# Two transformer layers on one core: the exchange of routed rows in two stages, the first during the output projection

## The chip, the core and the metric

The kernel runs on one NeuronCore of a Trainium2 chip. The core has five engines, each with its own in-order queue of instructions: PE (TensorE, matrix products; PEld is its weight load), DVE (VectorE), ACT (ScalarE), POOL (GpSimd) and SP (SyncE, which here only starts transfers). They wait for one another by semaphores, and 16 DMA engines move data between DRAM and on-chip memory. The metric is the device time of one execution in microseconds (us). Over three runs the kernel before took 4654.71 us in the median, from 4647.03 to 4658.94.

## The reference

Two equal layers over `x` of 2048 tokens by 1024 features, all in float32. A layer is attention and then a feed-forward network on eight routed tokens:

```python
def _A_ref(x, wqkv, wo):                     # attention, 32 heads of 32
    q, k, v = (x @ wqkv) split into heads
    p = softmax(einsum("bhqd,bhkd->bhqk", q, k) * 32 ** -0.5)
    return einsum("bhqk,bhkd->bhqd", p, v) merged @ wo

def _B_ref(x, w_r, w_gate, w_up, w_down):    # routed feed-forward
    r = x @ w_r                              # one score per token
    idx = argsort(-r)[:8]                    # the eight tokens with the highest score
    x_sel = x[idx]
    y = (silu(x_sel @ w_gate) * (x_sel @ w_up)) @ w_down * sigmoid(r[idx])
    return x with y added at the rows idx

x = x + _A_ref(_layernorm(x), ...);  x = x + _B_ref(_layernorm(x), ...)   # layer 1
x = x + _A_ref(_layernorm(x), ...);  x = x + _B_ref(_layernorm(x), ...)   # layer 2, same weights
```

So layer 2 needs all rows of layer 1, and eight of them only after layer 1's feed-forward network, which in turn can only begin when all 2048 scores are known.

## The kernel before, in words

**Products in halves.** TensorE works in a reduced type (fp32r) here. To keep accuracy each operand of the projections is split into a high half, a rounded copy made by ACT, and a low half, the operand minus its high half, made by POOL or DVE. Each product is three passes: high by high, low by high, high by low.

**One layer.** `layer(n, src, dst, prev)` is called with n = 0 and n = 1 (below: layer 1 and layer 2).

1. *Projection.* The tokens go in 4 chunks `c` of 512, the weight `wqkv` in 12 blocks `wb` of 256 columns (0 to 3 queries, 4 to 7 keys; 8 to 11 values, where a pair of blocks halves the sum). That gives 48 blocks and 96 half-block steps `k`; the first chunk takes the value blocks first, the others last. `load_w` fetches a raw block into `wraw`, `split_w` makes `wh` on ACT (line 584) and `wl` on POOL (line 585), two buffers of each. The loop emits the split of block j+1, and the load of block j+2, at the first step of block j (lines 741 to 745). A token tile of 128 rows is loaded by SP (`xt`), measured (`ln_stats`, lines 133 to 138) and normalised (`ln_norm`, line 599) on DVE and POOL, transposed by PE (line 612), and copied to `xh` by ACT (line 613) and `xl` by DVE (line 617). The products are line 634. ACT copies a query or key step's result out at line 648, a value block's at line 675, and DVE makes the low half after it.
2. *Attention.* 32 units (8 groups of 4 heads by 4 query chunks) of 16 key tiles each. The keys of the first group are fetched by `load_k`, at the steps that `KEYS_AT` names.
3. *Output projection.* 16 token tiles. `ord` (attention output and reciprocal sums), its halves `ohl`, and the split weights `woh` and `wol` feed 48 products per tile (line 991). Then DVE adds the residual, normalises, and reduces with `w_r` to the tile's column of scores (line 1019); POOL adds (line 1020), and SP stores the tile to `dst`.
4. *Routing.* During tile 15, `candidates` finds the best eight of the first 15 tiles; `route` adds the last tile's and settles the eight.
5. *Feed-forward.* Weight pieces of 1 MB (`fw`) are fetched by `load`, and `FeedForward.steps` holds 49 steps: gate (`g`) and up (`u`) products, 8 pieces each for two halves of the columns, transposes, 14 down products, and the sum `y`.

**Between the layers.** `dst` of layer 1 is a DRAM buffer, `x3`. Layer 2 must not wait for the feed-forward network. So `exchange` moves the routed rows out of the way: it works out which of the last eight rows are not routed themselves, gathers them and scatters them to the places of the routed rows further ahead (lines 240 and 241, through `gather`, line 199, and `scatter`, line 203). From then on the last eight rows of `x3` belong to the routed tokens, and only layer 2's last token tile waits for the network. Attention over all tokens does not depend on their order; at the end `back` moves rows to their own places, and `token` translates row numbers.

Layer 2's start is written out by hand: load two blocks of weights and the first three tiles, split block 0, five feed-forward steps with the gate's products held back (`hold`), statistics and norms, four more feed-forward steps, then transposes of tiles 0 and 1. In the loop, `k % 4 == 2` brings three more feed-forward steps (`tick`, which also sends off the loads that the steps before it have made room for), line 731. At k=60 the network is done and layer 2's last tile is loaded.

The order on each engine is the order in which the program emits, engine by engine; buffers of one name in a pool are reused in turn, and an instruction that needs a buffer waits until its earlier users are done.

Of the kernel before, what the change touches and what calls it, by code (L numbers as in the profile page):

```python
# [27 lines left out]


# [13 lines left out]
KEYS_AT = {(2, 23): slice(0, 3 * 512), (3, 3): slice(3 * 512, S)}  # L43
# [14 lines left out]
def tile_kernel(ctx, tc, x, wqkv, wo, w_r, w_gate, w_up, w_down, out):  # L58
# [49 lines left out]
    tail = cons.tile([128, 8], F32, name="tail")  # L108
    pool.iota(pos, pattern=[[128, NT]], base=0, channel_multiplier=1, allow_small_or_imprecise_dtypes=True)
    pool.iota(tail, pattern=[[1, 8]], base=S - 8, channel_multiplier=0, allow_small_or_imprecise_dtypes=True)  # L110
# [9 lines left out]
    pool.iota(last_c, pattern=[[0, 9]], base=S - 128, channel_multiplier=1, allow_small_or_imprecise_dtypes=True)  # L120
    ones16 = cons.tile([NT, 128], F32, name="ones16")
    pool.memset(ones16, 1.0)
    ones_c = ones16[0:8]
    PERM = {}
# [16 lines left out]
    class FeedForward:  # L141
# [5 lines left out]

        def __init__(self, n, dst, mrd):
            self.n, self.dst, self.mrd = n, dst, mrd
            self.stacks, self.pools, self.W, self.HT, self.t = [], [], {}, {}, {}  # L150
            self.todo, self.steps, self.free = [], [], []
            for h in range(2):
                for k in "gu":
                    self.steps += [(k, h, a) for a in range(KD)]
                self.steps.append(("t", h, 0))
            self.steps += [("d", 0, c) for c in range(14)] + [("y", 0, 0)]
            self.todo = [u for u in self.steps if u[0] in "gud"]
            self.lag, self.hold, self.late = 0, False, None
# [9 lines left out]
        def open(self):  # L168
# [4 lines left out]
            else:  # L173
                self.fx = self.push("fwa", 5, "right")
                self.pools = [(self.push("fwb", 4, "right"), "fw", 4)] * 4 + [(self.fx, "fw", 5)] * len(self.todo)
# [26 lines left out]
        def scatter(self, idx, in_):  # L202
            pool.indirect_dma_start(out=self.dst, out_offset=bass.IndirectOffsetOnAxis(ap=idx[:, :1], axis=0),
                                    in_=in_, in_offset=None)
# [4 lines left out]
        def exchange(self, sb, idx):  # L209


            tiny = self.tiny
            s, tcol = sb[:, 0:1], self.tcol
            lt, ne, ni, nit = tiny([8, 1], "lt"), tiny([8, 8], "ne"), tiny([8, 1], "ni"), tiny([8, 1], "nit")
            dve.tensor_scalar(lt, s, float(S - 8), None, op0=OP.is_lt)
# [4 lines left out]
            dve.tensor_tensor(nit, ni, tcol, op=OP.mult)  # L220
            p = ps_st()
# [4 lines left out]
            dve.tensor_scalar(eq, p[0:8, 8:16], d, None, op0=OP.is_equal)  # L226
            p = ps_st()
            pe.matmul(p[0:8, 0:1], eq, nit, start=True, stop=True)
            v = tiny([8, 4], "v")
# [7 lines left out]
            abi = PERM["ab"] = cons.tile([8, 2], I32, name="abi")  # L237
            dve.tensor_copy(abi, ab)
            tg = self.tmp.tile([128, D], F32, name="x", bufs=3)[0:8]
            self.gather(tg, abi[:, 0:1], self.dst)  # L240
            self.scatter(abi[:, 1:2], tg)
            dve.tensor_copy(v[:, 0:1], s)
            self.v = v

        def permutation(self):

            p = ps_st()
            for i in range(3):
                vb = small.tile([8, 128], F32, name="vb")
                pool.tensor_scalar(vb, ones_c, self.v[:, i:i + 1], None, op0=OP.mult)  # L250
                pe.matmul(p[:, 8 * i:8 * i + 8], vb, ident[0:8, 0:8], start=True, stop=True)
            bc = PERM["bc"] = cons.tile([128, 24], F32, name="bc")
            dve.tensor_copy(bc, p[:, 0:24])

        def back(self):

            rows, last = (self.tmp.tile([128, D], F32, name=i, bufs=k)[0:8] for i, k in (("x", 3), ("wrb", 1)))
            self.gather(rows, PERM["ab"][:, 1:2], self.dst)
            act.dma_start(last, self.dst[S - 8:S, :])
            self.scatter(PERM["ab"][:, 0:1], rows)  # L260
            self.scatter(PERM["routed"], last)

        def token(self, idx, s):

            a, b, bc = self.tiny([8, 1], "ta"), self.tiny([8, 1], "tb"), PERM["bc"]
            j = small.tile([8, 8], F32, name="tj")
            dve.scalar_tensor_tensor(j, bc[0:8, 0:8], s, bc[0:8, 8:16], op0=OP.is_equal, op1=OP.mult, accum_out=a)
            dve.scalar_tensor_tensor(j, tail[0:8], s, bc[0:8, 16:24], op0=OP.is_equal, op1=OP.mult, accum_out=b)
            dve.tensor_tensor(a, a, b, op=OP.add)
            dve.tensor_tensor(a, a, s, op=OP.add)  # L270
            dve.tensor_copy(idx, a)
# [46 lines left out]
        def route(self, rcols, xn, wp):  # L318


            n, tiny = self.n, self.tiny
            self.tmp = wp
            self.bg = bg = wp.tile([128, D], F32, name="x", bufs=3)[0:8] if n else self.fx.tile([8, D], F32, name="bg", bufs=1)
            xs = self.xs = (self.fs if n else self.fx).tile([128, KD, 32], F32, name="xs", bufs=1)
            pool.memset(xs, 0.0)
            if not n:
                self.tcol = tiny([8, 1], "tcol")
                pool.tensor_scalar(self.tcol, pos[0:8, 0:1], float(S - 8), None, op0=OP.add)
# [5 lines left out]
            mx, mi, mif = tiny([1, 8], "mx"), tiny([1, 8], "mi", U32), tiny([1, 8], "mif")  # L334
# [5 lines left out]
            pick = tiny([128, 2, 8], "pick2")  # L340
# [3 lines left out]

            def tokens():
                p = ps_st()
                pe.matmul(p[0:8, 0:9], pl, last_c, start=True, stop=False)
                pe.matmul(p[0:8, 0:9], pc, self.ca, start=False, stop=True)
                if not n:
                    pe.matmul(p[0:8, 16:24], last_c[:, 0:8], pl, start=True, stop=False)  # L350
                    pe.matmul(p[0:8, 16:24], self.ca[:, 0:8], pc, start=False, stop=True)
                sb = tiny([8, 24], "sb")
                for sl in (slice(0, 9), slice(16, 24))[:2 - n]:
                    dve.tensor_copy(sb[:, sl], p[0:8, sl])
                idx = tiny([8, 1], "idx", I32) if n else cons.tile([8, 1], I32, name="routed")
                dve.tensor_copy(idx, sb[:, 0:1])
                self.gather(bg, idx, self.dst)
                return sb, idx

            if not n:  # L360
                sb, PERM["routed"] = tokens()
                self.exchange(sb, idx=PERM["routed"])
# [7 lines left out]
            if n:  # L370
                sb, idx = tokens()
                self.back()
                self.tok = tiny([8, 1], "tok", I32)
                self.token(self.tok, sb[:, 0:1])
# [3 lines left out]
            dve.reciprocal(sg, sg)  # L378

        def row_tile(self):  # L380
            return self.tmp.tile([128, D], F32, name="xn", bufs=1) if self.n else self.fx.tile([128, D], F32, name="fy", bufs=1)

        def gate(self):
            if self.late:
                e, g = self.late
                self.late = None
                dve.tensor_scalar(e, e, 1.0, None, op0=OP.add)
                dve.reciprocal(e, e)  # L388
                pool.tensor_tensor(e, g, e, op=OP.mult)

        def step(self):
# [6 lines left out]
            if k in "gu":  # L398
# [6 lines left out]
                if a == KD - 1:  # L405
                    acc = self.acc
                    if k == "g":
# [4 lines left out]
                        self.late = (e[:m], g[:m])  # L412
                        if not self.hold:
                            self.gate()
# [23 lines left out]
            else:  # L438
# [5 lines left out]
                if self.n:  # L444
                    self.scatter(self.tok, self.bg)
                else:
                    dma(self.dst[S - 8:S, :], self.bg)
# [4 lines left out]
        def tick(self):  # L452
            for _ in range(self.lag):
                self.load()
            self.lag = self.step()

        def finish(self):
            while self.steps:
                if self.step():
                    self.load()  # L460
            self.close()

        def close(self):
# [3 lines left out]
            if self.n:  # L467
                self.end.close()

    def layer(n, src, dst, prev=None):  # L470
# [6 lines left out]
        mrd = dram.tile([S, 2], F32, name=f"mrd{n}")  # L477
# [83 lines left out]
        with ExitStack() as pst:  # L561
# [16 lines left out]
            def split_w(parts=1):  # L578
                wb, raw = RAW.pop(0)
                wh, wl = (pr_.tile([128, 2048], F32R, name=i) for i in ("wh", "wl"))  # L580
                W[wb] = [w.rearrange("p (a c) -> p a c", a=KD if wb < 8 else 4) for w in (wh, wl)]
                for i in range(parts):
                    sl = slice(2048 // parts * i, 2048 // parts * (i + 1))
                    act.copy(wh[:, sl], raw[:, sl])  # L584
                    pool.tensor_tensor(wl[:, sl], raw[:, sl], wh[:, sl].bitcast(F32), op=OP.subtract)  # L585
                    yield

            def ln_load(t):
                XT[t] = pr_.tile([128, D], F32, name="xt", bufs=3)
                dma(XT[t], src[t * 128:(t + 1) * 128, :])  # L590
# [10 lines left out]
            def ln_tr(t, wide=True):  # L601
                c, i = divmod(t, 4)
                if i == 0:
                    XC[c] = (pw.tile([128, KD, 512], F32R, name="xh"), pw.tile([128, KD, 512], F32R, name="xl"))
                xh, xl = XC[c]
                sl = slice(i * 128, (i + 1) * 128)
                ps = [(slice(0, KD), ps_pre())] if wide else [(slice(4 * j, 4 * j + 4), ps_st()) for j in range(2)]
                ps = [(asl, p.rearrange("p (a c) -> p a c", c=128)) for asl, p in ps]
                for asl, p in ps:
                    for j in range(asl.stop - asl.start):  # L610
                        a = asl.start + j
                        pe.transpose(p[:, j, :], XT[t][:, a * 128:(a + 1) * 128], ident)
                    act.copy(xh[:, asl, sl], p)

                def low():
                    for asl, p in ps:
# [445 lines left out]
```

## Time and profile before

One profiled execution took 4656.52 us, and its span from the first to the last instruction was 4654.5 us. All durations below are of this execution.

| what | value |
| --- | --- |
| median of three runs | 4654.71 us (4647.03 to 4658.94) |
| profiled execution / its span | 4656.52 / 4654.5 us |
| busy share PE, PEld | 98%, 58% |
| busy share DVE, POOL, ACT | 68%, 69%, 52% |
| mean granted TensorE clock | 0.987 |
| layer 1: projection from / first scores / last output product | 15.6 / 600.7 / 2246.7 us |
| layer 2: projection from / first scores / output projection done | 2287.84 / 2905.75 / 4552 us |

How such rows are read: a row of the timeline has the start in us, the duration, the engine, the line of the program, the operation, "out<-in" with the names of the buffers, the shapes, and "xN" where N instructions of one kind were put together; in square brackets stands how long the engine was idle before it and what released it. "SPq" is a transfer started by SP. Names such as `pre`, `st` and `pv` are the accumulators in PSUM.

### The profile page before, as it was taken

What the parts mean: (1) busy time and instruction counts of PE and PEld (TensorE: products, weight loads), DVE (VectorE), ACT (ScalarE), POOL (GpSimd) and SP (SyncE); (2) the same over time, 40 slices, a digit from 0 to 9 for tenths busy, and PEclk for the clock granted to TensorE, in tenths of its full rate; (3) what the DMA queues carried; (4) which work ended last, traced back from release to release, by engine and by line L of the source; (5) the groups of instructions that cost most, each with busy time, mean ns of one, the idle gap of its engine ahead of it and who ended that gap; (6) DMA issues with size and microseconds to landing.
All of it is one profiled execution on the core that took longest, in us unless ns stands there. A gap on an engine that the chain in (4) does not pass through costs nothing. (4 is left out here: it accounts for less than half of the span.)

```text
span 4654.5 us, 73388 instructions
## 1 busy us (share of the span) xinstructions
PE 4542.4 (98%) x29228; PEld 2697.7 (58%) x29228; DVE 3185.8 (68%) x4899; ACT 2428.1 (52%) x2562; POOL 3212.2 (69%) x1233
## 2 busy tenths in 40 slices
PE   8999999999999999999899999999999999999996
PEld 7887755545555555548577777555555555554572
DVE  2211578888888888876522215888888888887763
ACT  3222266767667676760122222776767667677400
POOL 4444378989889898944433442888889889898441
PEclk9999999999999999999899999999999999999997
DMA  5756476867777777749578674777767768676598
GB/s 184 201 179 196 141 165 145 180 149 161 170 153 168 156 168 158 181 118 262 180 247 288 218 208 128 162 168 155 172 148 171 160 150 180 147 168 159 149 257 309
DMA packets 326598, 833.26 MB, mean 179 GB/s; under 512 B 43008, under 2 KB 158720, under 8 KB 277088
## 3 DMA queue, kind: packets, MB, share of 16 engines
q1 hardware_dynamic: 272720, 476.91, 34.5%
q0 software_dynamic: 45024, 325.41, 34.5%
q10 hardware_dynamic: 8512, 26.26, 2.1%
q8 instruction: 229, 3.75, 0.3%
q14 instruction: 113, 0.93, 0.1%
HBM read 384.14 MB, written 119.24 MB: 108 GB/s over the span
## 5 line engine op out<-in xcount | busy, mean ns | idle before, releaser
L531 DVE TENSOR_REDUCE nm<-st 128x1 f32<-128x512 f32 x3916 | 2433.8, 684 | 373.4 <-PE st L523 367.4
L878 ACT ACTIVATE P<-pre 128x1024 f32<-128x1024 f32 x2048 | 1985.8, 1022 | 719.7 <-PE pre L538 521.9
L814 POOL TENSOR_TENSOR acc<-acc,P 128x2048 f32<-128x2048 f32 x434 | 2105.5, 4851 | 87.3 <-DMA P<-P 80.3
L538 PE MATMUL pre<-q,ks 64*128 64x512 f32 (+1 forms) x8192 | 1138.3, 395 | 4.2 <-ACT P L878 4.2
L804 PE MATMUL pv<-P,v 128*32 128x512 f32 x8192 | 1091.4, 605 | 4.5 <-DMA v<-vd 4.5
L523 PEld LDWEIGHTS st<-ks,q 64*128 64x128 f32 x3916 | 546.8, 184 | 907.5 <-DVE nm L531 764.2
L523 PE MATMUL st<-ks,q 64*128 64x512 f32 x3916 | 986.5, 471 | 0.4
L585 POOL TENSOR_TENSOR wl<-wraw,wh 128x2048 fp32r<-128x2048 f32 (+1 forms) x97 | 442.7, 4564 | 653.6 <-ACT wh L584 645.1
L538 PEld LDWEIGHTS pre<-q,ks 64*128 64x128 f32 (+1 forms) x8192 | 772.8, 187 | 186.6 <-ACT P L878 57.3
L817 POOL DMA_DIRECT2D P<-P x310 | 298.4, 963 | 257.5 <-PE st L523 185.0
L649 DVE TENSOR_TENSOR lo<-st,hi 128x512 fp32r<-128x512 f32 x128 | 88.5, 692 | 566.1 <-ACT hi L648 547.6
L634 PE MATMUL st<-xh,wh 128*128 128x512 f32 x1024 | 410.0, 400 | 0.0
L634 PE MATMUL st<-xh,wl 128*128 128x512 f32 x1024 | 402.0, 393 | 4.4 <-POOL wl L585 4.4
L634 PE MATMUL st<-xl,wh 128*128 128x512 f32 x1024 | 403.1, 394 | 0.0
L648 ACT CAST hi<-st 128x512 fp32r<-128x512 f32 x128 | 75.1, 586 | 538.7 <-PE st L634 533.6
L804 PEld LDWEIGHTS pv<-P,v 128*32 128x32 f32 x8192 | 162.3, 108 | 260.7 <-issue 252.5
L814 POOL TENSOR_TENSOR acc<-P 128x2048 f32<-128x2048 f32 x62 | 295.2, 4762 | 9.7 <-ACT P L878 5.2
L991 PE MATMUL pre<-woh,ohl 128*128 128x512 f32 x1024 | 245.5, 398 | 18.8 <-DVE pre L1019 13.2
L584 ACT CAST wh<-wraw 128x2048 fp32r<-128x2048 f32 (+1 forms) x97 | 183.2, 1891 | 148.2 <-PE pre L634 71.2
L991 PEld LDWEIGHTS pre<-woh,ohl 128*128 128x128 f32 x1024 | 195.3, 192 | 66.8 <-issue 17.2
L634 PEld LDWEIGHTS st<-xh,wh 128*128 128x128 f32 x1024 | 193.1, 189 | 56.4 <-issue 8.9
L634 PEld LDWEIGHTS st<-xh,wl 128*128 128x128 f32 x1024 | 193.3, 189 | 46.5 <-POOL wl L585 5.2
(249 smaller groups left out, 2961.7 us busy)
## 6 DMA issues: line engine op xcount, KB each, us to landing
P<-P POOLq DMA_DIRECT2D x310, 1024.0 KB, 8.9
wraw<-in_A_wqkv_dram SPq DMA_DIRECT2D x96, 1024.0 KB
q<-qh SPq DMA_DIRECT2D x256, 128.0 KB
ks<-kh SPq DMA_DIRECT2D x112, 256.0 KB
vd<-vn SPq DMA_DIRECT2D x32, 512.0 KB
qh<-hi SPq DMA_DIRECT2D x64, 256.0 KB
ql<-lo SPq DMA_DIRECT2D x64, 256.0 KB
kh<-hi SPq DMA_DIRECT2D x64, 256.0 KB
```

The source lines that it names most:

```text
L523: pe.matmul(ps[b], Q[u][rows, i, 0, qt * 128:(qt + 1) * 128], KS[(u // QC) % 2][rows, i, 0, j * 512:(j + 1) * 512], start=True, stop=True, ...
L531: dve.tensor_reduce(NM[u][:, j, 2 * i + b:2 * i + b + 1, qt], ps[b], axis=AX.X, op=OP.max, negate=True)
L538: pe.matmul(p[:, b * 512:(b + 1) * 512], KS[(u // QC) % 2][rows, i, slot, kt * 128:(kt + 1) * 128], Q[u][rows, i, slot, :], start=(slot == ...
L584: act.copy(wh[:, sl], raw[:, sl])
L585: pool.tensor_tensor(wl[:, sl], raw[:, sl], wh[:, sl].bitcast(F32), op=OP.subtract)
L634: pe.matmul(p, *pair(a, l, r), start=(a == 0 and k == 0), stop=(a == KD - 1 and k == 2))
L649: dve.tensor_tensor(lo, p, hi.bitcast(F32), op=OP.subtract)
L804: pe.matmul(PV[u][32 * h:32 * h + 32, :], V[g][:, kt, 32 * h:32 * h + 32], P[s][:, h, :], start=(kt == 0), stop=(kt == NT - 1), tile_posit ...
L814: (dve if on_dve else pool).tensor_tensor(o, a, P[u * NT + k].rearrange("p h c -> p (h c)"), op=OP.add)
L817: pool.dma_start(P[u * NT + a], P[u * NT + b], accum_op=OP.add)
L878: act.activation(P[s][:, 2 * i:2 * i + 2, :].rearrange("p h c -> p (h c)"), p, AF.Exp, scale=SCALE)
L991: pe.matmul(p[:, bl], l[:, a, :], r[a][:, bl], start=(k == 0 and a == 0), stop=(k == 2 and a == KD - 1))
```

## The change

1. *Two stages.* `x3` and the array of row statistics are split into two DRAM buffers at row CUT = 1272. The first stage (`first_stage`) selects the best eight among tiles 0 to 9 while tiles 10 to 13 of layer 1's output projection are computed, moves rows so that the last eight rows of the first part belong to these candidates, and copies them to the front of the second part. The second stage (`second_stage`) selects among those eight and tiles 10 to 15 and moves rows within the second part; it runs in layer 2's loop, one piece per step from k=3. `candidates` and `route` are left to layer 2.
2. *Layer 2's prologue inside layer 1.* `layer` becomes a generator. Layer 1 gets layer 2 as `following` and advances it at fixed points of its output projection: weight loads, four tile loads, statistics and norms, the split of block 0, transposes of tiles 0 and 1. For this `ord`, `ohl` and `woh` stand in a pool `wf` that outlives the output projection, and in layer 2 `split_w` takes `ord` and `ohl` as its two halves and chunks 0 and 2 of the transposed tokens take `woh`.
3. *The loop.* At k=0 in layer 2 the split and the load are left out; the prologue has split block 0 and loaded blocks 0 to 2. The splits from k=2 on take the raw blocks in order, 47 in all for 48 blocks; the last block multiplies with what the list of split weights holds under its number from the chunk before. Feed-forward steps start at k=10, four at every fourth step, with loads sent off one step later too (`refill`); the hold on the gate is gone.
4. *The three smaller changes:* `KEYS_AT` fetches the first three quarters of the keys in three parts; in layer 1 the first half of the split of block 0 is emitted ahead of the first transposes; at the end `back` is in two parts, the second stage's after the routing and the first stage's after ten steps of the network.

The core of the diff:

```diff
-KEYS_AT = {(2, 23): slice(0, 3 * 512), (3, 3): slice(3 * 512, S)}
+KEYS_AT = {(2, 14 + 3 * i): slice(i * 512, i * 512 + 512) for i in range(3)}
+KEYS_AT[3, 3] = slice(3 * 512, S)
...
+        def first_stage(self, rcols):
...
+            yield from self.stage(0, rcols[:, 0:CT], CT)
+
+        def second_stage(self):
+
+            yield from self.stage(1, self.rcols[:, CT:NT], NT - CT, self.front)
...
+            tg = self.scratch[0:8, 0:D]
+            self.gather(tg, abi[:, 0:1], dst)
+            self.scatter(abi[:, 1:2], tg, dst)
...
             def split_w(parts=1):
                 wb, raw = RAW.pop(0)
-                wh, wl = (pr_.tile([128, 2048], F32R, name=i) for i in ("wh", "wl"))
+
+                wh, wl = (prev.wf.tile([128, 2048], F32R, name=i) for i in ("ord", "ohl")) if n else (
+                    pr_.tile([128, 2048], F32R, name=i) for i in ("wh", "wl"))
...
             if n:
+                yield
                 load_w(8)
                 load_w(9)
...
+                yield
+                for t in range(4):
+                    ln_load(t)
+                yield
+                first_w = split_w()
+                next(first_w)
+                yield
+                for t in range(2):
+                    ln_stat(t)
+                    ln_norm(t)
+                yield
+                list(first_w)
+                load_w(blocks[2][1])
+                yield
+                ln_stat(2)
+                ln_norm(2)
+                yield
+                for t in range(2):
+                    ln_tr(t, False)()
+                    ln_load(t + 4)
+                yield
+                ln_stat(3)
+                ln_norm(3)
...
                     if k == 1:
-                        prev.hold = False
-                        prev.gate()
-                    if k % 4 == 2:
-                        for _ in range(3):
+                        yield
+                        pst.callback(prev.wf_end.close)
+                        pw = pst.enter_context(sbuf(f"pj{n}", bufs=2))
+                        routing = prev.second_stage()
+                    if k >= 3:
+                        next(routing, None)
+                    if k % 4 == 2 and k >= 10:
+                        for _ in range(4):
                             prev.tick()
-                    if k == 4:
-                        prev.permutation()
+                    if k % 4 == 3:
+                        prev.refill()
+                    if k in (13, 17):
+                        prev.permutation(k // 17)
...
                 j = k // 2 + 1
                 if i == 0 and j < len(blocks):
-                    list(split_w())
-                    if j + 1 < len(blocks):
+                    if not (n and j == 1):
+                        list(split_w())
+                    if j + 1 < len(blocks) and not (n and j == 1):
                         load_w(blocks[j + 1][1])
...
+                if nxt and t == CT:
+                    first_stage = ffn.first_stage(rcols)
                 for k, (l, r) in enumerate(((oh, woh), (ol, woh), (oh, wol))):
                     for a in range(KD):
...
+                        if first_stage and k == 2 and (a == 6 or a == 0 and t > CT):
+                            next(first_stage, None)
+                        if nxt and t >= NT - 3 and (k, a) == (2, 0):
+                            next(nxt)
...
+                if nxt and t == NT - 1:
+                    next(nxt)
                 x2 = X.pop(t)
...
+                if nxt and t >= NT - 2:
+                    next(nxt)
                 mv, rs = ln_stats(x2)
...
+                if nxt and t in (CT, NT - 3):
+                    next(nxt)
```

429 lines of the change are left out of this document (269 added, 160 removed).

## The prediction

> **What bounds the kernel now.** I read the page first (busy shares), then the busy time of each stretch around the seam of the two layers, then the waits of PE in layer 2's projection, then instructions in order of time at the seam and at a few block ends.
>
> ```profile
> PE 4542.4 (98%) x29228; PEld 2697.7 (58%) x29228; DVE 3185.8 (68%) x4899; ACT 2428.1 (52%) x2562; POOL 3212.2 (69%) x1233
> ...
> 2240.00:2290.00 50.00, 32.96 (x184) 20.81 (x183) 25.66 (x69) 6.91 (x7) 19.63 (x21) 0.73 0.48 174
> 2290.00:2340.00 50.00, 44.41 (x216) 32.75 (x216) 14.32 (x14) 9.99 (x11) 20.42 (x10) 0.93 0.64 235
> 2340.00:2740.00 400.00, 397.75 (x1881) 308.77 (x1881) 89.03 (x126) 110.09 (x113) 158.74 (x58) 1.00 0.74 240
> ```
> PE is busy 98% of the span; no other engine comes near. In the stretches (columns: length, busy time of PE, PEld, DVE, ACT, POOL, then the granted clock, DMA share, GB/s) PE loses 17 us and a quarter of its clock from 2240 to 2290, between the layers, and nearly nothing from 2340 to 2740, layer 2's projection. So there are about 25 to 40 us to win at the seam, and everything in the projection works only while PE never waits there.
>
> The seam:
>
> ```profile
> 2224.12 7.42 PE L991 MATMUL pre<-woh,ohl 128*128 128x512 f32 x32
> ...
> 2232.29 1.23 DVE L1019 SCALAR_TENSOR_TENSOR pre<-xn,wrb 128x1024 f32<-128x1024 f32 x1
> 2233.53 2.39 POOL L1020 TENSOR_TENSOR x<-x,xn 128x1024 f32<-128x1024 f32 x1
> 2234.99 5.38 PE L991 MATMUL pre<-woh,ohl 128*128 128x512 f32 x23
> ...
> 2243.16 0.27 PE L281 MATMUL st<-ident,rcols 128*15 128x128 f32 x1
> ...
> 2245.49 1.20 PE L991 MATMUL pre<-wol,ohl 128*128 128x512 f32 x4
> ...
> 2264.47 0.86 POOL L199 DMA_INDIRECT x<-x,abi  x1 [0.80 <-DVE x L363]
> 2269.86 0.90 POOL L203 DMA_INDIRECT x<-x,abi  x1 [4.52 <-DMA x<-x,abi]
> 2272.34 1.29 SPq L74 DMA_DIRECT2D xt<-x  x3
> 2272.60 9.47 PE L403 MATMUL pv<-fw,xs 128*32 128x512 f32 x64 [0.32 <-DVE sg L377]
> 2275.91 1.29 DVE L133 BATCH_NORM_STATS2 bst<-xt 128x6 f32<-128x512 f32 x2 [3.13 <-DMA xt<-x]
> 2287.84 0.51 PE L634 MATMUL pre<-wh,xh 128*128 128x512 f32 x1 [1.54 <-DVE xl L617]
> 2294.49 4.49 POOL L585 TENSOR_TENSOR wl<-wraw,wh 128x2048 fp32r<-128x2048 f32 x1
> 2294.55 4.97 DVE L599 TENSOR_SCALAR xt<-xt,mv,rs 128x1024 f32<-128x1024 f32 x1 [0.93 <-POOL rs L138]
> 2299.58 1.97 PE L612 MATMUL st<-ident,xt 128*128 128x128 f32 x8 [5.07 <-DVE xt L599]
> ...
> 2308.51 2.78 PE L403 MATMUL pv<-fw,xs 128*32 128x512 f32 x24
> 2311.23 0.50 PE L634 MATMUL pre<-wh,xh 128*128 128x512 f32 x1
> 2311.56 0.40 PE L634 MATMUL pre<-wl,xh 128*128 128x512 f32 x1
> ```
> Layer 1's last output matmul ends at 2246.7; the exchange's gather, scatter and the load of x3 follow one another to 2275.91; nine feed-forward steps run in the wait; the first matmul of layer 2 starts at 2287.84 and, after a stall for the fourth tile, its second block of weights at 2311.23.
>
> What keeps PE fed from there is that ACT and POOL split block j+1 while PE multiplies block j:
>
> ```profile
> 2322.03 0.39 PE L634 MATMUL pre<-wh,xl 128*128 128x512 f32 x1
> 2322.46 1.07 ACT L675 COPY vn<-pre 128x512 f32<-128x512 f32 x2 [4.36 <-PE pre L634]
> 2323.42 1.92 ACT L584 CAST wh<-wraw 128x2048 fp32r<-128x2048 f32 x1
> 2325.42 4.60 POOL L585 TENSOR_TENSOR wl<-wraw,wh 128x2048 fp32r<-128x2048 f32 x1 [1.99 <-ACT wh L584]
> 2334.92 2.78 PE L403 MATMUL pv<-fw,xs 128*32 128x512 f32 x24
> ...
> 2641.75 0.58 ACT L648 CAST hi<-st 128x512 fp32r<-128x512 f32 x1 [4.85 <-PE st L634]
> 2642.24 1.90 ACT L584 CAST wh<-wraw 128x2048 fp32r<-128x2048 f32 x1
> 2644.22 4.62 POOL L585 TENSOR_TENSOR wl<-wraw,wh 128x2048 fp32r<-128x2048 f32 x1 [4.26 <-ACT wh L584]
> ...
> 2655.58 1.02 ACT L613 CAST xh<-pre 128x1024 fp32r<-128x1024 f32 x1 [0.29 <-PE pre L612]
> 2658.47 4.61 POOL L585 TENSOR_TENSOR wl<-wraw,wh 128x2048 fp32r<-128x2048 f32 x1 [9.64 <-ACT wh L584]
> ```
> The last matmul of a block starts at 2322.03; ACT copies its result out (L675), then splits (L584), then POOL makes the low half (L585), done at 2330.02. PE needs it at 2334.9: 4.9 us to spare, one block ahead.
>
> **The change, part by part.**
>
> *The split loses its lead.* This decides the time. In layer 2 the prologue splits block 0, the loop's split at k=0 is left out, and so the split at the head of step k=2 takes block 1's raw weights from the list, the block that this very step multiplies. From then on every split stands directly before its own matmuls. In the order of instructions on ACT it follows the copy-out of the previous block's second half and precedes the copy-out of its own first half; on PE the first matmul of a block waits for ACT and the second for POOL. (47 splits are left of 48; the last block takes the older entry of its number and waits for none.) Each such block therefore exposes the whole chain. From the rows, second matmul to second matmul:
> - after a query or key block: the copy-out starts at 2641.75, 0.04 after the matmul's end, which started 0.4 earlier; POOL ends at 2648.84; undisturbed, the second matmul would start two spacings (0.46) after that last one, at 2641.77. Delay 7.1.
> - with a transposed tile's copy between (L613): 2663.08 against 2655.61 in that place, 7.5.
> - after a value block: 2330.04 against 2322.49, 7.55.
>
> Two value blocks of each chunk (the second of a pair, which has no copy-out before it) escape: their split follows the previous split directly, and two buffers suffice. In the first chunk block 3 does not, because POOL has the second stage's gathers before it (about 7.5, from 0.94 and 0.86 of gathers, 0.6 of small matmuls, and 4.6), and block 4 waits for gather, landing, scatter and split: 2264.47 to 2269.86 to 2275.3 with L228 before, 12.2. Where four feed-forward steps stand before the block (k=10, 14, ... 58), PE has 4 x 0.93 (2.78 for three) to do: 7.1 - 3.7, 3.5 left. In two of these the gate's work stands before the split on both engines:
>
> ```profile
> 2303.27 3.35 DVE L388 RECIPROCAL fy<-fy 128x512 f32<-128x512 f32 x1
> 2306.70 1.29 POOL L389 TENSOR_TENSOR fy<-fy 128x512 f32<-128x512 f32 x1 [7.72 <-DVE fy L388]
> ```
> copies 1.2 on ACT, then reciprocal and product on DVE and POOL before POOL's split: about 10 and 8. Counted over the four chunks: 13 x 7.1 + 8 x 7.5 + 6 x 7.55 + 7.5 + 12.2 + 9 x 3.5 + 18 = 267 us in 40 places. Bounds: without the small sums between (only wl, 4.6 each, less cover) 160; with 1 us more of semaphores and queueing at each place 310. I take 267, since three rows give the same chain.
>
> *The clock.* After a stall PE is slow for a while:
>
> ```profile
> 461.08 0.50 PE L634 MATMUL st<-xh,wl 128*128 128x512 f32 x1 [1.94 <-POOL wl L585]
> 464.67 0.55 PE L634 MATMUL st<-xh,wl 128*128 128x512 f32 x1
> ...
> 2768.83 0.67 PE L634 MATMUL st<-xh,wl 128*128 128x512 f32 x1 [2.44 <-POOL wl L585]
> 2772.28 0.46 PE L634 MATMUL st<-xh,wh 128*128 128x512 f32 x1
> 2772.57 0.39 PE L634 MATMUL st<-xh,wl 128*128 128x512 f32 x1
> ```
> Stalls of 1.94 and 2.44 us were followed by matmuls 0.43 apart in place of 0.23, until 464.9 and 2772.5: 7 and 8 of them, 1.5 and 1.7 us lost. After the 5.07 us at 2299.58 it was slow until 2304.8, 2.2 lost. So 31 long places at 2.2 and 9 short ones at 1.6: 83 us. Bounds: none, and 2.6 at each, 104. [...]
>
> *The seam itself.* Out projection: the selection leaves tile 15 (11.7 us, 2234.99 to 2246.7, where others take 10.87), -0.8; the first stage's ten small matmuls (0.2 to 0.38 each, pipelined, 2.2) and two waits for DVE on tiles 11 and 12 (its last reduction ends 9.5 us into a tile, 2233.5 against 2224.12; PE asks at 10.0, and 2.1 and 1.3 us of small operations stand between: 1.5 and 0.9) come into tiles 10 to 13, +4.6. So tile 15 starts at 2239.6. POOL's scatter waits for its gather as at 2264.47 to 2269.86, with tile 13's statistics behind it on POOL (0.9 late); SP's load of x3 waits for the scatter, with tile 15's input and tile 13's store behind it (both early enough). By the same rows as before (11.44 from gather to the first tile's arrival) tile 0 lands 1.5 us into tile 15. DVE, in order, stands there for it: statistics and norms of tiles 0 and 1 (2.4 and 2.9 of work and POOL waits), the second beside POOL's first split, as at 2294.55, +4.2; only then tile 14's residual, statistics, norm and reduction, tile 2's norm, and the low halves of tile 0: 23.4 us into tile 15. PE, done at 10.9, waits for these, 12 us; runs four half blocks in cold and warm clock to about 39.6; and waits for POOL's split of block 1, which stands behind tile 15's own tail, to 47.0. That is 2286.6 against 2311.56: -25. Bounds: -35 (DVE's waits overlap) and 0. Twelve feed-forward steps done by then before are done later: 12 x 0.93, +11. Second stage, its eight transposes and the two permutations on PE: about 25 small matmuls of 0.13 to 0.3, +4.
>
> *Small ones.* Keys fetched in three parts, a few steps earlier: the two stalls quoted above follow the old burst; without them layer 1 gains 3.4 and layer 2 4.1 (bounds 0 and that). Layer 1's first split moves ahead of the first copies on ACT: 2 (0 to 3.6, PE's first two waits). Layer 2's operands lie in other pools; layer 1's matmuls are 0.2336 apart and layer 2's 0.2270 (the rows above, 0.23), so another place may cost 2304 x 0.0066, 15; I take 0. At the end the second give-back stands on POOL between the two gates, which leaves it 15 us idle: 0, and up to 3 if it runs over.
>
> Sum: 4654.5 - 25 + 11 + 4 + 267 + 83 - 4.1 - 3.4 - 2 = 4985. The profiled execution lay 2.0 above its span and 1.8 above the median, so on the median's footing 4985.
>
> **The rivals.**
> 1. *The other side:* the splits run ahead after all, because ACT and POOL find their buffers free and take them before the copy-out. Place: ACT, between two copy-outs; it decides as soon as a split starts before the copy-out that stands before it. Then 4654.5 - 25 + 11 + 4 - 9.5 = 4635, faster. For it: two buffers are free a block earlier. Against: in every row quoted the split follows the copy-out, and all three engines run in order. 0.03.
> 2. *Only ACT's part shows:* POOL's split is ready in time and just the copy-out and 1.9 us are exposed, 31 x 2.5 with 1.6 of clock at each: 4765. Against: POOL cannot start before ACT's half, and PE's second matmul reads the low half. 0.05.
> 3. *The clock stays up:* 4985 - 83 = 4902. Against: the rows at 461 and 2768. 0.06.
> 4. [...] 0.14. [...]
> 5. *Raw weights late as well:* in 13 blocks three feed-forward loads stand before the next raw block on SP, and wait for PE.
>
> ```profile
> 2325.78 10.59 SPq L190 DMA_DIRECT2D fw<-in_B_w_gate_dram  x2
> ```
> Here two of them held SP 10.59 us. 4 MB at 240 GB/s, 17 us behind 3.7, against about 19 to the split: 4 us late at each, 5037. 0.13.
>
> The forecast has 0.59.
>
> **How the numbers follow.** 4985 is the likeliest case; its own range, 4935 to 5035, comes from the bounds of the 267 and the 83. 4900 to 5055 takes in cases 3 to 5 and the unknowns that add (seam without gain 25, other pools 15), and leaves out 1, 2 and some tail. Faster by over 0.3% (14 us, about what can be told from no change here): case 1, 0.03; same 0.01; slower 0.96.
>
> **What would show it.** Right: PE in layer 2's projection waits some 40 times for POOL's low half (4.5 each where uncovered, about 160 in all) and some 30 times about 2.5 for ACT's high half, the granted clock there falls from 1.00 to near 0.85, and the stretch from first projection matmul to first score grows from 611 us by more than 300. The seam: first projection matmul of layer 2 between 2255 and 2270. Wrong: splits that start before the copy-out; waits for POOL under 2 us; a seam that ends later than 2311.

## The result, and the profile after

The changed kernel took 4996.43 us in the median of four runs (4991.34 to 4999.43), the kernel before beside it 4656.82 (4647.03 to 4663.25): 1.0733 times the time, 95% interval 1.0719 to 1.0746. The forecast was 4985, between 4900 and 5055. The profiled execution took 4999.43, its span is 4997.4.

The head of the page of the changed kernel: busy time, share of the span, number of instructions.

```profile
PE 4629.7 (93%) x29224; PEld 2752.0 (55%) x29224; DVE 3183.0 (64%) x4945; ACT 2425.1 (49%) x2567; POOL 3208.1 (64%) x1246
```

Nearly the same instructions, but PE is idle for 368 us of the span in place of 112, and busy 87 us longer with them. Where that lies is told by the first and last products of each stage in the two profiled executions:

| stretch | before, us | changed, us | difference |
| --- | --- | --- | --- |
| start to first product of layer 1 | 15.61 | 13.77 | -1.8 |
| layer 1's projection | 578.75 | 570.78 | -8.0 |
| layer 1's output projection | 186.65 | 195.85 | +9.2 |
| from there to layer 2's first product | 41.15 | 12.55 | -28.6 |
| layer 2's projection | 611.57 | 977.61 | +366.0 |
| last output product of layer 2 to the end | 102.16 | 105.53 | +3.4 |
| the two attentions, layer 2's output projection | | | +2.7 |

Each row is of one execution. The same code gives the projections again to within 2 us in the profiles below, but layer 1's output projection took 195.85 us here and 203.00 in experiment 8, where the kernel is the same; so its row says little about the change. (The rows "first scores" of the table of before, 600.7 and 2905.75, are the first products with the values. The first products of keys and queries that follow the projections stand at 594.6 and 2899.7, and the 611 us of the forecast counts to these.)

The seam is shorter, as it should be, and layer 2's projection eats that thirteen times over. The busy time of each engine in that stretch (length, then PE, PEld, DVE, ACT, POOL, the granted clock, DMA share, GB/s), first before, then changed:

```profile
2288.00:2899.00 611.00, 600.71 (x2797) 462.01 (x2798) 175.64 (x220) 156.31 (x161) 229.91 (x78) 0.99 0.68 218
```
```profile
2260.00:3237.00 977.00, 708.64 (x2908) 519.83 (x2907) 182.63 (x276) 155.26 (x168) 230.22 (x91) 0.85 0.44 144
```

ACT and POOL do the same amount of work; PE is idle for 268 us where it was idle for 10, and the clock granted is 0.85. The list of PE's waits in the changed kernel (what it waited for: us in total, times, longest), from 2250 to 3230, says for whom:

```profile
PE st L759 <- POOL ohl L696: 141.9, 35, 7.1
PE st L759 <- ACT ord L693: 66.8, 26, 3.0
PE pre L759 <- POOL ohl L696: 38.3, 8, 7.1
PE pre L759 <- ACT ord L693: 16.2, 6, 3.0
PE st L730 <- DVE woh L738: 9.6, 1, 9.6
PE st L348 <- DVE fw L345: 2.4, 1, 2.4
```

L693 and L696 are the two halves of the split. PE waited 180.2 us, 43 times, for the low half and 83.0 us, 32 times, for the high half. One such place in order of time:

```profile
2987.05 0.39 PE L759 MATMUL pre<-ord,woh 128*128 128x512 f32 x1
2987.52 1.07 ACT L800 COPY vn<-pre 128x512 f32<-128x512 f32 x2 [4.36 <-issue]
2988.48 1.91 ACT L693 CAST ord<-wraw 128x2048 fp32r<-128x2048 f32 x1
...
2990.44 0.50 PE L759 MATMUL st<-xh,ord 128*128 128x512 f32 x1 [3.00 <-ACT ord L693]
2990.47 4.50 POOL L696 TENSOR_TENSOR ohl<-wraw,ord 128x2048 fp32r<-128x2048 f32 x1 [21.85 <-ACT ord L693]
...
2995.02 0.79 PE L759 MATMUL st<-xh,ohl 128*128 128x512 f32 x1 [4.08 <-POOL ohl L696]
2995.61 0.63 PE L759 MATMUL st<-xl,ord 128*128 128x512 f32 x1
2996.04 0.63 PE L759 MATMUL st<-xh,ord 128*128 128x512 f32 x1
...
2998.14 0.39 PE L759 MATMUL st<-xl,ord 128*128 128x512 f32 x1
2998.37 0.40 PE L759 MATMUL st<-xh,ord 128*128 128x512 f32 x1
```

The chain is all there: the previous block's last product at 2987.05, copy-out, high half, first product, low half, second product at 2995.02, that is 7.5 us later than the 2987.51 that two spacings would give. POOL had been idle for 21.85 us before its half: it had time for this split a block earlier and was not asked. Then the products start 0.43 apart in place of 0.23, for 3 us.

### The profile page after: what moved, and what is told of

Its sections match the earlier page's. It is cut to its first block, busy times and chain, and to the rows that moved or that the text cites. A ratio compares the mean times of both kernels' runs of the same rounds, so it can differ in the third digit from the quotient of the medians.

```text
span 4997.4 us, 73519 instructions
## 1 busy us (share of the span) xinstructions
PE 4629.7 (93%) x29224; PEld 2752.0 (55%) x29224; DVE 3183.0 (64%) x4945; ACT 2425.1 (49%) x2567; POOL 3208.1 (64%) x1246
## 5 line engine op out<-in xcount | busy, mean ns | idle before, releaser
L696 POOL TENSOR_TENSOR ohl<-wraw,ord 128x2048 fp32r<-128x2048 f32 x47 | 211.7, 4507 | 561.5 <-ACT ord L693 561.4
L696 POOL TENSOR_TENSOR wl<-wraw,wh 128x2048 fp32r<-128x2048 f32 (+1 forms) x49 | 221.7, 4524 | 315.5 <-ACT wh L693 315.5
L144 POOL TENSOR_TENSOR rs<-mv,eps_c 128x1 f32<-128x1 f32 x64 | 12.6, 197 | 313.6 <-DVE mv L142 313.5
L759 PE MATMUL st<-woh,ord 128*128 128x512 f32 x512 | 183.0, 435 | 28.1 <-ACT ord L693 28.1
L759 PE MATMUL st<-xh,wh 128*128 128x512 f32 x512 | 203.1, 397 | 0.0
L759 PE MATMUL st<-xl,wh 128*128 128x512 f32 x512 | 202.0, 394 | 0.0
L759 PE MATMUL st<-xh,wl 128*128 128x512 f32 x512 | 200.7, 392 | 0.0
```

The lines of the kernel that those rows point to most:

```text
L759: pe.matmul(p, *pair(a, l, r), start=(a == 0 and k == 0), stop=(a == KD - 1 and k == 2))
```

## The experiments

They ran apart from the result above, 1 to 4 on one chip and 5 to 9 on another, always beside the kernel before, which took 4666.8 to 4669.6 us there in the median. So ratios are compared, and stretches of the profiled executions.

**1. Give the lead back.** The changed kernel, with this edit:

```diff
-                    if not (n and j == 1):
-                        list(split_w())
+                    list(split_w())
```

> The changed kernel with the split of block 1 emitted at k=0 of layer 2 again, so that all 48 splits are there and each stands one block ahead of its products. Theory (the lost lead costs the time): layer 2's projection falls from 977.6 us back to about 611.6 + 11 for the feed-forward steps that moved into it + 4 for the second stage = 627 or a little less, and the whole goes to about 4640 us, below the kernel before. Rival A (the splits cannot run ahead because their new buffers come free too late): it stays above 4900. Rival B (part of the growth comes from four feed-forward steps at once and their late loads): between 4680 and 4850.

Measured: 4668.63 us, 0.9995 times the kernel before (0.9985 to 1.0005). The changed kernel has 1.0716 (experiment 8), so 0.072 of the time of before, about 337 us, is gone; the lost lead is what costs, and rivals A and B are out: with the new buffers the splits run ahead, and the feed-forward steps in fours come with no long wait. But the 15 us or more below the kernel before, which the theory promised, did not come. Layer 2's first product stayed early, at 2259.23, and its projection took 641.9 us in place of 627. The three largest of PE's waits from 2235 to 2430 in this version:

```profile
PE st L348 <- DVE fw L345: 11.4, 1, 11.4
PE st L730 <- DVE woh L738: 9.6, 1, 9.6
PE st L357 <- POOL vb L356: 8.3, 4, 4.0
```

L348 are the second stage's eight transposes and L357 the products of the two permutations, both in the middle of the projection. They are short, but PE takes them in order and waits for what stands ahead of their inputs on POOL and DVE:

```profile
2312.79 0.87 POOL L208 DMA_INDIRECT fw<-x,ab  x1 [5.45 <-DVE abs L325]
2319.89 0.89 POOL L212 DMA_INDIRECT x<-fw,ab  x1 [6.23 <-DMA fw<-x,ab]
2320.81 4.50 POOL L696 TENSOR_TENSOR ohl<-wraw,ord 128x2048 fp32r<-128x2048 f32 x1
2325.26 0.19 POOL L144 TENSOR_TENSOR rs<-mv,eps_c 128x1 f32<-128x1 f32 x1
2326.13 0.81 DVE L711 TENSOR_SCALAR xt<-xt,mv,rs 128x1024 f32<-128x1024 f32 x1 [11.89 <-POOL rs L145]
2327.71 0.80 DVE L345 TENSOR_SCALAR fw<-bg,mg 8x1024 f32<-8x1024 f32 x1
2328.57 1.02 PE L348 MATMUL st<-ident,fw 8*128 8x8 f32 x8 [11.38 <-DVE fw L345]
```

POOL's scatter waits 6.23 us for its gather to land; the split of the next block and tile 4's statistics stand behind it; DVE stands in tile 4's norm for 11.89 us, with the row for the transposes behind that; and PE stands with it. Steps 8, 9, 12, 13, 16 and 17 took 33 us more than in the kernel before, slow products after the waits and three of the moved feed-forward steps among them. In the changed kernel itself the same transposes waited 2.4 us: PE was late there anyway.

**2. Take the lead away from the kernel before**, and nothing else:

```diff
-                    list(split_w())
+                    if not (n and j == 1):
+                        list(split_w())
```

> The kernel before with one edit: in layer 2 the split at k=0 is left out, so that the later splits stand directly before their own products; the last block then uses the older entry of its number, that block's own weights are left out. Theory: the seam stays at 2287.8, layer 2's projection grows from 611.6 by about 250 of waits and 75 of slow clock, to about 935, and the whole to about 4980 us. PE's waits there are for the low half (about 4.3 each) and the high half (about 2.5 each). Rival (the new pools, the second stage or the moved feed-forward steps carry most of it): below 4750.

Measured: 5001.11 us, 1.0711 times the kernel before (1.0693 to 1.0729). Layer 2's projection took 942.15 us, 330.6 more than before. PE's waits there:

```profile
PE st L634 <- POOL wl L585: 142.5, 35, 6.9
PE st L634 <- ACT wh L584: 67.6, 27, 3.0
PE pre L634 <- POOL wl L585: 22.9, 6, 4.1
PE pre L634 <- ACT wh L584: 13.2, 5, 3.0
```

246 us of waits, where about 250 had been expected, without the pools, the second stage or the moved steps. So the split left out at k=0 makes the whole of the loss; all the rest of the change together comes to nothing, as the first experiment says from the other side.

**3. Fill the waits with useless products.** The changed kernel, with products that nobody reads ahead of each late block:

```diff
+                if n and i == 0 and 4 <= k < 88 and k not in (46, 66, 70):
+                    fill = ps_st()
+                    cnt = 12 if 10 <= k <= 58 and k % 4 == 2 else 28
+                    for q in range(cnt):
+                        pe.matmul(fill, xpart(c, 0, 0)[:, 0:128], xpart(c, 0, 0), start=(q == 0), stop=(q == cnt - 1))
```

> The changed kernel with useless products on PE (28, or 12 where feed-forward steps stand before) ahead of each late block in layer 2's projection up to k=86; their result is read by nobody. They use time in which PE would wait for the split. Theory (waits and a slow clock after each wait are two costs, some 70 to 80 us are the clock's): the time falls by 45 to 75 us, to about 4920 to 4950, and products after the split are 0.23 apart at once. Rival (the slow products are the cost of something else, such as POOL and ACT reading on-chip memory at the same time): no fall, 4995 to 5030.

Measured: 4946.89 us, 1.0596 (1.0579 to 1.0614); the changed kernel has 1.0716 (experiment 8), so some 56 us went by giving PE more to do. The same stretch as above in this version:

```profile
2261.00:3183.00 922.00, 847.23 (x3807) 643.48 (x3806) 182.69 (x276) 155.78 (x168) 233.36 (x91) 0.96 0.48 153
```

900 products more and the clock granted rose from 0.85 to 0.96, with nearly the same busy time of POOL (233.36 us against 230.22) and ACT (155.78 against 155.26): the slow products went with PE's own idleness, not with what its neighbours do. Counted in the traces, products 0.3 to 0.9 us apart cost 87.7 us more than 0.227 each in the changed kernel's layer 2 projection, 8.4 in the kernel before's, 34.0 here, where 39 of the 43 places were filled.

**4. The keys alone.** The kernel before with the fetch in three parts:

```diff
-KEYS_AT = {(2, 23): slice(0, 3 * 512), (3, 3): slice(3 * 512, S)}
+KEYS_AT = {(2, 14 + 3 * i): slice(i * 512, i * 512 + 512) for i in range(3)}
+KEYS_AT[3, 3] = slice(3 * 512, S)
```

> The kernel before with the fetch of the keys in three parts alone. Theory: the two stalls for POOL's low half at 461 and 2769 go, 3.8 us in layer 1 and 4.3 in layer 2, so 4646.5 us in all and no other step of the projections changes. Rival (the lower time of layer 1's other steps, 0.1 us each in the changed kernel, comes with the fetches too): 4640 or less. Rival (the fetch only moves the stall): 4654.

Measured: 4660.93 us, 0.9987 (0.9977 to 0.9996). Layer 1's projection fell from 578.75 to 575.00, layer 2's from 611.57 to 606.92; step 76 carries it, 9.36 to 5.60 us in layer 1 and 9.76 to 5.44 in layer 2, and products elsewhere kept their distance. So the stalls came with the fetch of three quarters in one piece. The whole fell by 0.0013 of its time, about 6 us, in place of the 8.4 of the two stretches. The fetch does not explain the further 4.2 us by which layer 1's projection is shorter in the changed kernel.

**5. Ease the second stage.** The version of experiment 1 with two edits:

```diff
             self.gather(tg, abi[:, 0:1], dst)
+            if i:
+                yield
             self.scatter(abi[:, 1:2], tg, dst)
...
-                    if k in (13, 17):
-                        prev.permutation(k // 17)
...
+                if prev and k in (13, 17):
+                    prev.permutation(k // 17)
                 if norm and at % 4 == 2:
```

> The changed kernel with all splits one block ahead, and two further edits: the second stage's scatter is emitted one step after its gather (so the piece with the transposes comes at k=10 in place of 9), and the two permutations come at the end of steps 13 and 17 in place of their beginning. Theory (the seam's gain was given back by PE waiting 11.4 us for the second stage's row, 8.3 us for the permutation's products from POOL, and about 9 us of slow clock after these): layer 2's projection falls from 641.9 to 611 to 618 us, and the whole by 24 to 31 us against the version with the lead alone, to a ratio of 0.9930 to 0.9950 to the kernel before. Rival (these waits only show what POOL and DVE have too much of, and come back at the next steps): the projection stays above 632.

Measured: 4644.23 us, 0.9947 (0.9931 to 0.9964): faster than both kernels, than the one before by half a per cent. Layer 2's projection took 617.3 us, 24.6 less than in experiment 1. The same three waits from 2235 to 2430 are:

```profile
PE st L732 <- DVE woh L740: 8.9, 1, 8.9
PE st L350 <- DVE fw L347: 2.4, 1, 2.4
PE st L359 <- POOL vb L358: 0.8, 2, 0.4
```

So the waits did not come back elsewhere, and they and the slow products behind them were what had taken the seam's gain. The two edits were made together; which of them brought how much isn't shown.

**6. The late split in pieces.** The changed kernel with

```diff
-                        list(split_w())
+                        list(split_w(4 if n else 1))
```

> The changed kernel, its late splits in four pieces each (a quarter on ACT, the same quarter on POOL, and so on), still directly before their own products. Theory (PE waits for the length of the chain copy-out, high half, low half): the chain to the first products shrinks from 0.6 + 1.9 + 4.6 to 0.6 + 0.5 + 1.2 and PE then follows the pieces, so some 40 waits become about 4.5 us shorter, layer 2's projection falls from 977.6 to 770 to 830 us and the whole to about 4800 to 4860 on this chip. Rival (PE waits for a whole block's halves, or the splits are late for a reason in front of them, such as raw weights): no fall by more than 40 us.

Measured: 4791.36 us, 1.0263 (1.0246 to 1.028). Layer 2's projection took 767.4 us, 210 less; this and the whole lie just below the ranges expected. The waits for the two halves fell from 263 to 92 us, and slow products, by the count of experiment 3, from 87.7 to 58.5. The same kind of place:

```profile
2850.46 0.39 PE L759 MATMUL st<-xl,ord 128*128 128x512 f32 x1
2850.88 0.58 ACT L773 CAST hi<-st 128x512 fp32r<-128x512 f32 x1 [4.85 <-PE st L759]
2851.36 2.18 ACT L693 CAST ord<-wraw 128x512 fp32r<-128x512 f32 x4
...
2852.04 0.49 PE L759 MATMUL st<-xh,ord 128*128 128x512 f32 x1 [1.19 <-ACT ord L693]
2852.06 5.01 POOL L696 TENSOR_TENSOR ohl<-wraw,ord 128x512 fp32r<-128x512 f32 x4 [8.48 <-ACT ord L693]
...
2853.38 0.50 PE L759 MATMUL st<-xh,ohl 128*128 128x512 f32 x1 [0.85 <-POOL ohl L696]
2853.72 0.40 PE L759 MATMUL st<-xl,ord 128*128 128x512 f32 x1
```

The split is still late, but PE starts after the first quarter, and the delay is 2.5 us (2853.38 against 2850.92) in place of 7.1. So the wait goes with the length of the chain, and nothing ahead of the chain held it up.

**7. The place of layer 1's operands.** The kernel before with

```diff
-            pr_ = pst.enter_context(sbuf(f"pw{n}", bufs=2, side=None if prev else "right"))
+            pr_ = pst.enter_context(sbuf(f"pw{n}", bufs=2, side=None))
```

> The kernel before with the pool of layer 1's weight blocks and token tiles on the other side of the on-chip memory, as layer 2 has it; nothing else. Theory (where the operands lie sets the 0.2336 between layer 1's products, against 0.2270 in layer 2): layer 1's projection falls from 579 to about 564 us, the whole by 15 us. Rival (it is something else of layer 1): no change, 575 to 580 us.

Measured: 4656.48 us, 0.9974 (0.9964 to 0.9983). Layer 1's projection took 562.95 us, 15.8 less; the whole gained 0.0026 of its time, about 12. The same moment of it before and with the edit:

```profile
59.91 0.40 PE L634 MATMUL pre<-wh,xl 128*128 128x512 f32 x1
60.14 0.40 PE L634 MATMUL pre<-wh,xh 128*128 128x512 f32 x1
60.38 0.40 PE L634 MATMUL pre<-wl,xh 128*128 128x512 f32 x1
```
```profile
59.98 0.39 PE L634 MATMUL pre<-wh,xh 128*128 128x512 f32 x1
60.21 0.39 PE L634 MATMUL pre<-wl,xh 128*128 128x512 f32 x1
60.43 0.39 PE L634 MATMUL pre<-wh,xl 128*128 128x512 f32 x1
```

Over whole steps of 24 products the distance went from 0.234 to 0.227 us, at the same granted clock (1.00).

**8. The changed kernel again**, on the chip of experiments 5 to 9:

> The changed kernel itself, beside the others on this chip. Both theories: 1.072 to 1.075 times the kernel before, and layer 2's projection at 977 us.

Measured: 5004.02 us, 1.0716 (1.0698 to 1.0734); layer 2's projection took 977.67 us. Its interval overlaps that of the first comparison, and layer 2's projection is the same to 0.1 us as in the result.

**9. Experiments 5 and 7 together.**

> The version with the lead and the eased second stage, and layer 1's weight pool on the other side, as in the placement experiment. Theory (the two gains lie in different stretches and add): layer 1's projection goes from 572 to about 562 us, less than the 16 us of the placement alone since half of the chunks were already at 0.229, layer 2's stays at 617, and the ratio to the kernel before goes from 0.9947 to about 0.9925. Rival (layer 1's earlier end is taken by a wait at the output projection or the seam): 0.9945 to 0.9960.

Measured: 4638.99 us, 0.9939 (0.9921 to 0.9957). The profile has layer 1's projection at 562.4 us, 9.8 less than in experiment 5, as expected; but layer 2's took 619.2 and the tail 106.5, 1.9 and 3.6 more than there, so that the two spans are alike (4636.6 and 4636.9). The ratio lies between the two expectations. It is faster than the kernel before; that it is faster than experiment 5 isn't shown.

## Why the prediction was right, point by point

*The split loses its lead.* Forecast 267 us in 40 places; the two kinds of wait came to 263 us, in 43 and 32 pieces. The form was right too: about 40 waits for the low half, 4.2 us each, and about 30 of 2.6 for the high half. The total of the low half's was put at 160 and is 180, because a wait behind feed-forward steps falls on the low half. Experiments 1 and 2 show the cause from both sides, and 6 its mechanism.

That 263 meets 267 so closely is in part luck. The forecast counted a place from second product to second product; so measured, each place costs about 0.4 us more than its waits, and the 43 together about 282. The price of a place was good: the whole chain came to 6.98 to 7.5 us where nothing else stood between (forecast 7.1 and 7.55), eight of the places behind four feed-forward steps to about 3.5 (3.5), and the two with the gate's work to 10.3 and 7.6 (10 and 8). Block 4 came to 10.4 (12.2). What was off is mainly their number, 43 in place of 40.

*The clock.* Forecast 83 us; counted 79 (87.7 less the 8.4 of before), and 54 of these are gone in experiment 3, which did not reach all places. The forecast's two classes were only roughly right. In the changed kernel the 35 stops of 4.7 us or more (both waits of a place taken together) were each followed by 7 to 14 slow products, 1.9 us lost beside the first one's 0.4. Of the eight between 3.0 and 3.5 us, only two were. So "1.6 us at each short place" was too much.

How long a stop must be to cost the clock, the traces answer only in part. Over the projections of all eleven profiles, take the stops of 0.3 us or more right before a projection product (both waits of a place taken together, layer 1's first product left out): none of 37 stops under 1.5 us was followed by five or more slow products, 32 of 68 between 1.5 and 4.7 us were, 13 of 27 between 2.0 and 2.6 us in experiment 6 alone among them, and all 110 above. So 2.0 to 2.6 us were enough in some places, as 2.44 us at 2768.83 in the kernel before, and 3.06 to 3.48 us were not at six of the changed kernel; what else decides, no run here shows.

*The seam.* Forecast for the second product of block 1: 2286.6, 25 us earlier; it came at 2282.12, 29.4 earlier. Of these 9.8 are layer 1's shorter start and projection, so attention, output projection and seam together gave 19.6, and the forecast was 5 us too good. The wait of 12 us for DVE was 9.6, the one for POOL's split of block 1 was there, 7.1. What it missed is in the output projection, priced at +3.8. The +9.2 of the one pair isn't its measure, since the stage varies too much: 186.65 to 196.53 us in the four profiles that leave it as it was (before and experiments 2, 4 and 7), 192.38 to 203.00 in the seven with the change. Its tiles 11 to 15 alone tell the two apart: 55.96 to 57.82 us in the four, 63.37 to 66.37 in the seven, 8.2 more in the mean. The forecast's waits and products in tiles 11 and 12 are there and larger: these two took 28.2 to 29.5 us in place of 22.5 to 24.4. What it did not have is a wait of PE of 1.2 to 2.2 us for DVE at the end of tile 14, which is 1.4 to 2.4 us longer in all seven. The first ten tiles, 118.6 to 126.2 us in the four and 116.8 to 125.6 in the seven, show no cost of the change; why they vary so stays open.

*Feed-forward steps and second stage*, +11 and +4. A half-block step with four feed-forward steps takes 9.10 us in the changed kernel, with three 8.24 in the kernel before: 0.86 for each that moved. The second stage's +4 could pass only because of the late splits. Here the prediction's reasoning fell: priced by its products, the second stage leaves out what stands ahead of them on POOL and DVE. Experiment 1 shows it as 19.7 us of waits, of which experiment 5 leaves 3.2; with the slow products behind them it got back 24.6 us. The rival "the other side" at 4635 was for this reason wrong in its price: with the splits ahead the kernel was not 20 us faster than before but equal.

*Small ones.* Keys: forecast -3.4 and -4.1; experiment 4 measured -3.7 and -4.7. Layer 1's first split: forecast -2; the first product came 1.8 us earlier, but the first two steps took 0.6 and 0.9 more, so -0.4 is left. The place of the operands: 0 was taken for layer 2, with 15 as the other end, and 0 held: a step that nothing disturbs takes 5.44 us there in both kernels. Layer 1 in the changed kernel gained 0.1 us in about half of its steps, 5.7 us in all, though its own pools are the same, and experiment 7 got the whole 15.8 by a move of one of them. The tail: 0 taken, 3 as the end, measured 3.4, and 1.5 in experiment 8.

*The rivals.* "The other side" did not come: in the place shown above the split starts at 2988.48, behind the copy-out at 2987.52. "Only ACT's part shows" falls by the 180 us of waits for POOL. "The clock stays up" falls by the granted clock of 0.85 and by experiment 3. The fourth, 0.14, turns on short stops: the clock held at six of the eight places between 3.0 and 3.5 us, but the 35 long ones lost 1.9 us each, and 79 us were counted in all. "Raw weights late as well" falls too: no wait of ACT for a raw block is in the list of waits of layer 2's projection in the changed kernel.

The sum of 4985 lay 11 us below the median. In the profiled pair the terms that were too small are the output projection (by 5.4, part of it scatter), the tail (3.4), layer 2's projection (366.0 against 361: 267, 83, 11 and 4 less 4.1) and, never counted, the attentions and the second output projection (2.7). Against them went the 5.7 us that layer 1's projection gained and that no term held.

## What to carry to other kernels

Before a change to a software pipeline is priced by what it moves, follow one producer through the order of instructions on each engine and count how many blocks lie between it and its reader: a lead of one lost at the start is lost at every block, and 30 us won at a seam stand against some 43 times 8. A few tiny instructions on the engine that bounds the kernel cost what stands ahead of their inputs on the other in-order engines (19.7 us of waits in experiment 1); put them where these are already done, and a transfer's reader one step after the transfer. Where PE must wait anyway, useless products can be cheaper than rest, as they were in experiment 3, by some 56 us.

## What the runs showed of the hardware that was not expected

- Moving one pool of buffers from one side of the on-chip memory to the other brought layer 1's products from 0.234 to 0.227 us apart, at the same granted clock: 15.8 us of 579. Why, no run shows.
- 900 products that nobody reads, in 39 places, made the changed kernel some 56 us faster.
- Stops of PE between 1.5 and 4.7 us were followed by five or more slow products in 32 cases of 68, shorter ones in none of 37, longer ones in all of 110: between 1.5 and 4.7 us the length of a stop alone did not decide whether it cost the clock.
